# A new order for all queues of a linear-attention layer with a gated MLP, and three dummy matmuls fewer

## The chip, the cores and the metric

The kernel runs on one core of a Trainium2 chip. The metric is the device time of one execution in microseconds (us). A core has five engines that run side by side, each through a queue of its own in order: PE (TensorE, matmuls; PEld is its weight load), ACT (ScalarE), DVE (VectorE), POOL (GpSimd) and SP (SyncE, which issues nearly all the DMAs here).

## The reference

Everything is bf16, with 2048 tokens of 448 features. A layer norm, then attention of 16 heads of 28 features without a token-by-token matrix, the output product and a residual; then a second layer norm and a gated MLP of width 1792 with a residual.

```python
qkv = (layernorm(x) @ wqkv)                       # q, k, v, 16 heads of 28
pq, pk = q @ w_phi[h], k @ w_phi[h]
phi_q = concat([softmax(pq), softmax(-pq)]); phi_k = concat([softmax(pk), softmax(-pk)])
kv, z = phi_k.T @ v, phi_k.sum(tokens)            # per head
o = (phi_q @ kv) / (phi_q @ z + 1e-6)
h = x + o @ wo
out = h + (sigmoid(hn @ w_gate) * (hn @ w_up)) @ w_down     # hn = layernorm(h)
```

## The kernel before

The work is cut into 16 tiles of 128 tokens. `build` records some 900 tasks, each with an engine (or a choice of two or three), the tasks it depends on, and a choice of PSUM banks; the recording order means nothing. A table, `ORDER`, then sets the order of all five queues: each of its numbers names a task (the number over 32), the choice of banks (the next bits) and the choice of engine (the last two). `stored` reads it:

```python
t = self.tasks[names[int(v) // 32]]
t.eng = t.engs[int(v) % 4]
...
t.got, gate = t.banks[int(v) // 4 % 8]
```

A task waits for its dependencies and for whoever last used its banks, by semaphores. `TURNS` adds waits that no data asks for: in each pair the first task also waits for the second, which keeps two tasks of different engines apart.

```python
for name, first in TURNS:
    self.tasks[name].need.append(first)
```

The stages, with the lines that the text speaks of:

- **Start.** `warm` and `fill` (L543, L1006) are dummy matmuls of 512 columns on zeros, which depend on nothing but a cleared tile. `NFILL` says how many there are, and the table where they stand. Four key transpositions on PE (L552) turn the raw key weights; copies (L437, `WkT`) bring them to SBUF; products with the feature weights (L568) fold `w_phi` into the key weights, and copies (`Wk`) bring these to SBUF. The query weights come as four raw loads (`wq_raw`), two DMA transpositions (L512, `WqT`) and the same folding (L568, then `Wq`).
- **First layer norm.** DVE takes statistics (L596, L598). A small step and a power on POOL (L599, L601) make the factor, and `xn_pad` (L614 on ACT, L616 on POOL, L617 on DVE) is the normalized x. Six tiles are transposed by PE (L627) and copied, the others by DMA (L635).
- **Key/value stage.** For each tile 14 + 14 matmuls of half the array (L655), in two tasks of 8 and 6; two exponentials on ACT (L675, L677) and a copy of v; sums and reciprocals (L685 on POOL or DVE, L691, L696, L700); features (L702, `phi`); and 16 short matmuls that add up the summary in bank 4 (L714). L721 starts that accumulation.
- **Query stage.** For each of 4 chunks of 512 tokens and 2 groups, 8 + 6 matmuls (L754) and two exponentials of 1024 columns (L764, `eq`).
- **Output stage.** When the summary is masked (`kvz`, L769), PE makes numerators and denominators of a tile in 16 short matmuls (L790), and ACT or DVE evicts them (L437, `opm`). For a pair of tiles follow, by their lines: reciprocal L806 and ratio L808 on DVE, a multiplication L810 and an addition L813 on `b_sb`, a reciprocal L816, the output multiplication L818 (`o_pad`), all of these big ones on DVE or POOL as the table says. The first pair is transposed by PE (L826, L828), the others get a small copy (L837) and a DMA transposition (L839). Then the output product (L851), the residual addition (L881; for the first pair a matmul adds x, L859, and two copies to `x_sb` follow), statistics (L876 and L878, or L885 and L887), the small step and the power on POOL (L889, L891), the normalization `hn_pad` (L895), and its transposition by PE (L905) or DMA (L913).
- **MLP.** Five token blocks of 2, 4, 4, 4 and 2 tiles. For each of 14 slices of the width, 7 gate and 7 up matmuls (L952), a tanh on ACT (L961), and a product on DVE (L969). Then 14 down matmuls a tile (L986), an addition (L993) and a store (L996).

PSUM has 8 banks. Gate and up, query and output products take pairs of them, so a task of PE also waits until the engines have read what the pair held before.

Of the kernel before, what the change touches and what calls it, by code (L numbers as in the profile page):

```python
# [30 lines left out]
SECOND = [(1, 0), (1, 1), (1, 2), (1, 3), (0, 0), (0, 1), (0, 3)]  # L31
NWARM = 1
KT_MM = 2
NFILL = 20

O_FIRST = [(0, 0), (0, 1), (0, 2), (0, 3), (1, 0), (1, 1), (1, 2)]
O_SECOND = [(1, 0), (1, 1), (1, 2), (1, 3), (0, 0), (0, 1), (0, 2)]
# [1 line left out]


ORDER = """
# [48 lines left out]
"""  # L90


TURNS = [(('Wp', 1), ('Wp', 0)), (('nm', 6), ('ve', 4)), (('mm', 4), ('ve', 4)), (('ve', 12), ('phi', 0)), (('mm',
# [5 lines left out]


class _Task:
# [4 lines left out]
class _Graph:  # L106
# [153 lines left out]
    def emit(self, rings):  # L260
        nc = self.nc
        done = self.stored(ORDER) if ORDER.strip() else self.order()
        for name, first in TURNS:
            self.tasks[name].need.append(first)
# [69 lines left out]
def build(nc, A_x, A_wqkv, A_w_phi, A_wo, B_w_gate, B_w_up, B_w_down, out):  # L334
# [19 lines left out]
    with ExitStack() as es:  # L354
# [649 lines left out]

        for i in range(NFILL):
            task(("fill", i), "pe", 0.22, lambda e: e.matmul(  # L1006
# [40 lines left out]
```

## Time and profile before

| | us |
|---|---|
| median of 3 runs | 204.57 (204.56 to 204.67) |
| the profiled execution | 204.33 |
| its span, first to last instruction | 202.4 |
| busy: PE / DVE / ACT / POOL | 197.8 / 130.4 / 94.1 / 55.0 |
| 20 dummy matmuls (L1006), busy | 8.0 |
| gate and up matmuls (L952), 980 | 175.2 |
| down matmuls (L986), 238 | 43.1 |

Matmuls overlap in the records, so the busy times of the lines add up to more than the stretch they fill. The chain of waits goes back from the last instruction and names at each step what released it. A timeline merges neighbours of one line; its columns are the start, the time from the first start to the last end, the engine, line and operation, and the count; in brackets the idle time ahead and what ended it. The rows that the prediction rests on stand there.

### The profile page before, as it was taken

The page shows a single profiled execution, that of the slowest core. Times are in us where ns is not written, and L with a number is a line of the kernel's source. Part 1 is how long each engine was busy: PE and PEld are TensorE (multiplying, and loading weights), DVE is VectorE, ACT ScalarE, POOL GpSimd, SP SyncE. Part 2 cuts the span into 40 slices and gives each one's busy share as a digit, 9 for nine tenths or more (in the row PEclk, how much of TensorE's full clock was granted, in tenths as well). Part 3 has the DMA queues.
Part 4 walks back from the last instruction along what each step waited for, and adds up shares of the span by engine and source line. Part 5 has one row for each costly group of instructions (what it writes and reads, how often), then busy time and mean ns, then how long its engine had stood idle before and what let it go on. Part 6 is the DMA issues. An engine that isn't in the chain of part 4 may idle for free.

```text
span 202.4 us, 5443 instructions
## 1 busy us (share of the span) xinstructions
PE 197.8 (98%) x2292; PEld 109.8 (54%) x2292; DVE 130.4 (64%) x295; ACT 94.1 (46%) x167; POOL 55.0 (27%) x81
## 2 busy tenths in 40 slices
PE   7999999999999999999999999999999999999994
PEld 2555555555457885555544444454444455896553
DVE  2999999997999898678724448752335224554222
ACT  2599999899998662424221323201352300442000
POOL 4689855442057414344330000300001000000000
PEclk9999999999999999999999999999999999999999
DMA  6996667863025395151371200083000211000111
GB/s 189 328 165 142 162 135 229 242 184 112 0 55 100 63 137 126 25 142 24 83 55 47 52 3 0 0 104 93 0 0 3 52 45 47 3 3 3 45 45 45
DMA packets 34052, 16.67 MB, mean 82 GB/s; under 512 B 25644, under 2 KB 33004, under 8 KB 34028
## 3 DMA queue, kind: packets, MB, share of 16 engines
q1 hardware_dynamic: 33676, 16.04, 34.9%
q8 instruction: 18, 0.29, 0.6%
q10 hardware_dynamic: 352, 0.29, 0.4%
q14 instruction: 6, 0.05, 0.1%
HBM read 8.98 MB, written 1.84 MB: 53 GB/s over the span
## 4 chain that ended last, share of the span: by engine, by line
PE 92%; DVE 2%; ACT 2%; POOL 1%; issue 0%; DVEq 0%
PE bank L952 42%; PE bank L986 21%; PE bank L655 11%; PE bank L851 5%; PE bank L754 4%; PE bank L1006 3%; ACT eq L764 2%; PE bank L714 2%; PE bank L790 1%; PE bank L568 1%; PE bank L627 1%; POOL b_sb L810 1%; PE bank L552 1%; DVE b_sb L813 1%; ACT opm L437 0%
## 5 line engine op out<-in xcount | busy, mean ns | idle before, releaser
L952 PE MATMUL bank<-xnT,wg_sb 64*128 64x512 bf16 (+1 forms) x490 | 87.6, 333 | 0.3 <-issue 0.3
L952 PE MATMUL bank<-xnT,wu_sb 64*128 64x512 bf16 (+1 forms) x490 | 87.6, 333 | 0.0
L961 ACT ACTIVATE sg_sb<-bank 128x512 f32<-128x512 f32 (+1 forms) x70 | 34.4, 512 | 81.2 <-PE bank L952 69.8
L969 DVE SCALAR_TENSOR_TENSOR hh<-sg_sb,bank 128x512 bf16<-128x512 f32 (+1 forms) x70 | 38.8, 576 | 28.3 <-ACT sg_sb L961 28.1
L952 PEld LDWEIGHTS bank<-xnT,wg_sb 64*128 64x128 bf16 x490 | 45.2, 94 | 19.0 <-issue 2.8
L952 PEld LDWEIGHTS bank<-xnT,wu_sb 64*128 64x128 bf16 x490 | 45.0, 94 | 16.8
L986 PE MATMUL bank<-wd_sb,hh 128*128 128x448 bf16 (+2 forms) x238 | 43.1, 342 | 0.0
L986 PEld LDWEIGHTS bank<-wd_sb,hh 128*128 128x128 bf16 x238 | 22.4, 98 | 20.7 <-issue 1.1
L993 DVE SCALAR_TENSOR_TENSOR x_sb<-bank,x_sb 128x448 bf16<-128x448 f32 (+2 forms) x17 | 10.1, 597 | 28.3 <-PE bank L986 28.3
L655 PE MATMUL bank<-Wk,xnT 64*128 64x448 bf16 x112 | 20.4, 350 | 0.0
L655 PE MATMUL bank<-Wv,xnT 64*128 64x448 bf16 x112 | 20.2, 350 | 0.0
L764 ACT ACTIVATE eq<-bank 128x1024 bf16<-128x1024 f32 x16 | 16.0, 1036 | 0.2
L889 POOL TENSOR_SCALAR rs<-mv 128x2 f32<-128x2 f32 x6 | 1.2, 193 | 52.3 <-DVE mv L887 48.7
L754 PE MATMUL bank<-xnT,Wq 64*128 64x512 bf16 x112 | 13.8, 376 | 0.3 <-ACT opm L437 0.3
L851 PE MATMUL bank<-wo_sb,oT 64*128 64x448 bf16 x112 | 13.3, 350 | 0.1
L437 ACT CAST opm<-bank 128x960 bf16<-128x960 f32 x13 | 12.2, 962 | 0.1
L818 POOL TENSOR_TENSOR o_pad<-b_sb,rden 128x896 bf16<-128x896 bf16 x5 | 8.4, 1689 | 12.1 <-DVE rden L816 9.2
L685 POOL TENSOR_TENSOR half_s<-ek 128x448 f32<-128x448 bf16 x10 | 9.7, 970 | 7.6 <-DVE phi L702 5.0
L655 PEld LDWEIGHTS bank<-Wk,xnT 64*128 64x128 bf16 x112 | 8.7, 94 | 5.2 <-issue 0.7
L596 DVE BATCH_NORM_STATS2 st<-x_sb 128x6 f32<-128x448 bf16 x16 | 9.1, 613 | 3.2 <-DMA x_sb<-in_A_x_dram 3.2
L655 PEld LDWEIGHTS bank<-Wv,xnT 64*128 64x128 bf16 x112 | 8.7, 94 | 4.5
L881 DVE TENSOR_TENSOR x_sb<-bank,x_sb 128x896 bf16<-128x896 f32 x7 | 7.6, 1089 | 3.7 <-PE bank L851 3.6
(99 smaller groups left out, 210.3 us busy)
## 6 DMA issues: line engine op xcount, KB each, us to landing
wg_sb<-in_B_w_gate_dram SPq DMA_DIRECT2D x4, 448.0 KB, 4.2
wu_sb<-in_B_w_up_dram SPq DMA_DIRECT2D x4, 448.0 KB, 3.6
out_dram<-x_sb SPq DMA_DIRECT2D x15, 112.0 KB, 1.7
wd_sb<-in_B_w_down_dram SPq DMA_DIRECT2D x7, 224.0 KB, 2.8
x_sb<-in_A_x_dram SPq DMA_DIRECT2D x2, 448.0 KB, 5.1
x_sb<-in_A_x_dram SPq DMA_DIRECT2D x3, 224.0 KB, 3.9
wq_raw<-in_A_wqkv_dram SPq DMA_DIRECT2D x4, 128.0 KB, 4.7
Wv<-in_A_wqkv_dram SPq DMA_DIRECT2D x2, 224.0 KB, 4.2
```

Of the source, the lines that this page charges most:

```text
L437: return e.copy(dst, src) if hasattr(e, "activation") else e.tensor_copy(dst, src)
L596: task(("bst", t), "dve", dve(D), lambda e, t=t: e.bn_stats(st1[:, t % 4, :], X(t)), [x_ld[t], opt(("agg", t - 4))])
L655: r = e.matmul(bank[bk][:, 0:D], lhsT=half(xnT, hi)[:, t, k, :], rhs=half(w, hi)[:, k, :], start=(i == 0), stop=(i == 6), tile_position=(6 ...
L685: task(("sa", t), None, 0.88, lambda e, t=t, s=s: e.tensor_tensor(half_s[:, t % NSA].rearrange("p (a n) -> p a n", a=4 * G), ek[:, s].rear ...
L754: r = e.matmul(bank[bb[j]], lhsT=half(Wq2, hi)[:, k, 2 * g:2 * g + 2].rearrange("p c d h -> p (c d h)"), rhs=half(xnT, hi)[:, 4 * c:4 * c ...
L764: task((key, gp, c), "act", act_p(1024), lambda e, gp=gp, c=c, sg=sg, nm=nm: e.activation(eq[c][:, sg, 2 * gp:2 * gp + 2, :], wide[got(nm) ...
L851: r = e.matmul(bank[bb[j]][:, 0:D], lhsT=half(oT, hi)[:, pr % NO, j, k, :], rhs=half(wo_sb, hi)[:, k, :], start=(i == 0 and not res), stop ...
L952: r = e.matmul(bank[b][:, 0:N], lhsT=half(w, hi)[:, k, fs], rhs=half(hnT, hi)[:, t0:t0 + n, k, :], start=(i == 0), stop=(i == 6), tile_pos ...
L961: task(("sig", f_, c), "act", act_p(N), lambda e, j=j, N=N, nm=nm: e.activation(sg_sb[:, j % NSG, 0:N], bank[got(nm)[0]][:, 0:N], ACT.Tanh ...
L969: task(("hh", f_, c), "dve", dve(N), lambda e, j=j, N=N, nm=nm, f_=f_, c=c: e.scalar_tensor_tensor(hhT[c % 2][:, f_, 0:N], sg_sb[:, j % NS ...
L986: r = e.matmul(bank[b][:, c0:c1], lhsT=hhT[c % 2][:, f_, o:o + P], rhs=wd_sb[:, f_, c0:c1], start=(f_ == 0), stop=(f_ == FT - 1))
L993: task(("fin",) + nm[1:], "dve", dve(c1 - c0), lambda e, nm=nm, tt=tt, pr=pr, c0=c0, c1=c1: e.scalar_tensor_tensor(X(tt)[:, c0:c1], bank[g ...
```

## The change

`NFILL` goes from 20 to 17, and the tables `ORDER` and `TURNS` are replaced as a whole. No task's own code changes. One line of the file goes, so that every line behind the tables has a number smaller by one after the change.

```diff
-NFILL = 20
+NFILL = 17
...
 ORDER = """
-448 0 736 544 224 1152 96 288 576 29120 608 480 28960 640 128 160 28576 800 256 28672 192 768 29024 704 28608
...
+128 448 0 736 544 224 160 1152 96 256 576 28768 608 192 384 480 28992 640 352 28544 768 28960 288 704 28832
...
-TURNS = [(('Wp', 1), ('Wp', 0)), (('nm', 6), ('ve', 4)), (('mm', 4), ('ve', 4)), (('ve', 12), ('phi', 0)), (('mm',
...
+TURNS = [(('Wp', 0), ('Wp', 1)), (('xn', 10), ('mm', 12)), (('sa', 6), ('sa', 4)), (('sa', 8), ('sa', 9)), (('sa',
+         10), ('phi', 9)), (('sa', 11), ('phi', 8)), (('phi', 13), ('phi', 11)), (('c', 0), ('b', 0)), (('b', 2),
+         ('od', 1)), (('b', 3), ('od', 2)), (('o', 3), ('hn', 2)), (('b', 5), ('od', 3)), (('rstd2', 2), ('ve2', 2)),
...
```

In `TURNS`, `b`, `c`, `o` and `od` are the multiplication, the addition, the output multiplication and the small copy of a pair of tiles, and `hn` a normalized tile; `(('b', 2), ('od', 1))` holds the third pair's multiplication until the second pair's copy is done.

What the table moves on the queues, at the places where the prediction speaks of it:

PE's queue where the last key/value tiles give way to the query groups, before (`xnT,Wq` is a query group, `v,phi` the summary, `kvz,eq` a tile's numerators):

```order
L754 MATMUL bank<-xnT,Wq 128x512 x8
L655 MATMUL bank<-Wk,xnT 128x448
L655 MATMUL bank<-Wv,xnT 128x448
L655 MATMUL bank<-Wk,xnT 128x448
L655 MATMUL bank<-Wv,xnT 128x448
L655 MATMUL bank<-Wk,xnT 128x448
L655 MATMUL bank<-Wv,xnT 128x448
L714 MATMUL bank<-v,phi 64x58 x16
L754 MATMUL bank<-xnT,Wq 128x512 x34
L714 MATMUL bank<-v,phi 64x58 x96
L754 MATMUL bank<-xnT,Wq 128x512 x8
L790 MATMUL bank<-kvz,eq 128x60 x32
```

The same place after the change:

```order
L654 MATMUL bank<-Wk,xnT 128x448
L654 MATMUL bank<-Wv,xnT 128x448
L753 MATMUL bank<-xnT,Wq 128x512 x36
L713 MATMUL bank<-v,phi 64x58 x16
L753 MATMUL bank<-xnT,Wq 128x512 x6
L713 MATMUL bank<-v,phi 64x58 x80
L753 MATMUL bank<-xnT,Wq 128x512 x8
L789 MATMUL bank<-kvz,eq 128x60 x32
```

Before, the first half of the group stood ahead of the last key/value half tile, and the run of 34 began with the 6 matmuls that end it. Now the run of 36 is 8 of the first group, 8 of the second, then the 6 that end the first, the 6 that end the second, and 8 of the third.

POOL's queue from the last features to the second power, before:

```order
L702 TENSOR_TENSOR phi<-ek,rsum 128x16x56
L810 TENSOR_TENSOR b_sb<-opm,rr 128x928
L818 TENSOR_TENSOR o_pad<-b_sb,rden 128x2x448
L889 TENSOR_SCALAR rs<-mv 128x2
L891 TENSOR_TENSOR rs<-rs,neghalf 128x2
L810 TENSOR_TENSOR b_sb<-opm,rr 128x928
L813 TENSOR_TENSOR b_sb<-b_sb,opm 128x928
L818 TENSOR_TENSOR o_pad<-b_sb,rden 128x2x448
L889 TENSOR_SCALAR rs<-mv 128x2
```

And after:

```order
L701 TENSOR_TENSOR phi<-ek,rsum 128x16x56 x2
L812 TENSOR_TENSOR b_sb<-b_sb,opm 128x928
L809 TENSOR_TENSOR b_sb<-opm,rr 128x928
L812 TENSOR_TENSOR b_sb<-b_sb,opm 128x928
L888 TENSOR_SCALAR rs<-mv 128x2
L890 TENSOR_TENSOR rs<-rs,neghalf 128x2
L809 TENSOR_TENSOR b_sb<-opm,rr 128x928
L812 TENSOR_TENSOR b_sb<-b_sb,opm 128x928
L888 TENSOR_SCALAR rs<-mv 128x2
```

The first pair's addition, and the third pair's multiplication and addition, now stand ahead of the first power; the first pair's multiplication and the third pair's output multiplication have gone to DVE.

DVE's queue from the first normalization of the output stage to the first residual addition, before:

```order
L895 TENSOR_SCALAR hn_pad<-x_sb,mv,rs 128x512 x2
L806 RECIPROCAL rSm<-opm 128x32
L437 COPY xnT<-bank 128x512 x2
L808 TENSOR_TENSOR rr<-rSm,opm 128x32
L881 TENSOR_TENSOR x_sb<-bank,x_sb 128x896
```

And after:

```order
L894 TENSOR_SCALAR hn_pad<-x_sb,mv,rs 128x512 x2
L817 TENSOR_TENSOR o_pad<-b_sb,rden 128x2x448
L807 TENSOR_TENSOR rr<-rSm,opm 128x32
L836 COPY o_pad<-o_pad 128x2x64
L436 COPY xnT<-bank 128x512 x2
L880 TENSOR_TENSOR x_sb<-bank,x_sb 128x896
```

The third pair's output multiplication and copy now come between the normalization and the copies of its transposed tiles. The two copies of the first pair to `x_sb`, which ACT made, are DVE's now.

Elsewhere: the clearings of the padding (L459, L460, L458, L468 and L469) and the mask of the summary (L464) now stand on POOL ahead of the first small step; all four folded key weights are copied by ACT, where one was DVE's; the small loads of the output weights and the stores stand later on SP.

101 rows, old and new, of tables (ORDER, TURNS) are left out of this document.

## The prediction

> **What bounds the kernel now.** I read the page first, then the waits of PE, then the chain of waits, and then the timelines of the stages in which the chain leaves PE.
>
> ```profile
> span 202.4 us, 5443 instructions
> PE 197.8 (98%) x2292; PEld 109.8 (54%) x2292; DVE 130.4 (64%) x295; ACT 94.1 (46%) x167; POOL 55.0 (27%) x81
> PE bank L754 <- ACT opm L437: 0.3, 1, 0.3
> PE bank L790 <- DVE opm L437: 0.2, 1, 0.2
> ```
>
> PE is busy for 98% of the span, and its waits after the first matmul add up to 0.8 us: these two, and one of 0.3 that term 4 shows. The real work of PE is the same in both versions, so the time after is the time before, less the dummies, less the waits that go, plus the waits that come. The profiled execution took 204.33 us, 1.93 us more than its span, and the median of the runs, 204.57, is 0.24 us above it. I sum against 204.33 and add 0.24.
>
> A busy PE hides how little slack its neighbours have. Three places hold PE up, or nearly: the arrival of the transposed query weights near 18 us, the first gate and up matmul at 61.59, and the second token block at 76.76.
>
> **Term 1, the dummies.** The first run of them shrinks from 12 to 11, those between the key transpositions and 20 us from 4 to 3, and those of the output stage (46 to 62 us) from 4 to 3.
>
> ```profile
> 1.44 5.30 PE L1006 MATMUL bank<-warm 128*128 128x512 bf16 x12
> 6.56 1.76 PE L552 MATMUL bank<-ident,wk_raw 128*128 128x128 bf16 x16
> 8.65 0.22 PE bank L1006
> L473 SPq DMA_DIRECT2D wk_raw<-in_A_wqkv_dram x1: 456/456/456, 1.3 to 1.3; - x1
> DMA to landing us min/median/max: 4.1/4.2/4.3
> ```
>
> The first 12 stand (6.56 - 1.44)/12 = 0.427 us apart; a later one costs 0.22. The key weights are there at 1.3 + 4.3 = 5.6 us, so PE begins the key transpositions 0.43 earlier, and all three dummies are worth at most 0.43 + 0.22 + 0.22 = 0.87 us. What is late next is this:
>
> ```profile
> L512 SPq DMA_TRANSPOSE WqT<-wq_raw x2: 1240/1291/1342, 12.0 to 15.5; - x2
> DMA to landing us min/median/max: 2.7/3.6/4.4
> 18.34 0.75 PE bank L568 x12
> 25.06 0.57 PE bank L655 x6
> 10.14 0.20 PE bank L721
> 9.52 0.20 PE bank L568 x4
> 22.41 0.30 PE bank L568 x4
> ```
>
> The second transposition of the query weights is issued at 15.5 and lands 2.7 later, at 18.2; the product that needs it starts at 18.34. In either order the last of their four raw loads stands behind both big x loads, and only one small row load of the output weights has gone from ahead of it, so I leave the landing where it is. Up to this product PE has nearly the same work behind it in both versions: the new order has the second half of a key/value tile more (0.57), one x transposition (four short matmuls: 0.20) and the accumulator's starting matmul (0.20) fewer, and carries one dummy (0.22) past it, +0.05 for what follows. PE therefore only comes earlier to a wait. **I take 0 for all three dummies** (the one of the output stage goes from a stretch in which PE waits anyway). The bounds are 0.87 gained, if every gate moves along, and 0.1 lost.
>
> **Term 2, the second query projection.** PE now runs both first halves of the next two query groups before it finishes the first.
>
> ```profile
> 40.38 3.84 PE L754 MATMUL bank<-xnT,Wq 64*128 64x512 bf16 x34
> 41.40 5.99 ACT L764 ACTIVATE eq<-bank 128x1024 bf16<-128x1024 f32 x6
> 47.39 2.70 ACT L437 CAST opm<-bank 128x960 bf16<-128x960 f32 x3
> ```
>
> Before, the six matmuls that end the first group are the head of the run at 40.38 (34 matmuls in 3.84 us: 0.11 each), so it is done at about 41.2, and ACT starts its exponentials at 41.40. Now 8 matmuls of another group (0.87) stand ahead of that end. On the way from 18.34 there are three fewer changes between matmuls of the half array and of the full one, at about 0.1 each (four products took 0.20 at 9.52 among their like, and 0.30 at 22.41 where such a change follows): -0.28. With the 0.05 of term 1, ACT starts its six exponentials at 41.2 + 0.87 - 0.28 + 0.05 = 41.85, **0.45 late**. They run back to back, so the evictions behind them start 0.45 late too. Bounds: 0.2 earlier, if the dummies' time survives, and 0.9 late, if the four summary matmuls that now stand in one block ahead of the first query's end wait for their features.
>
> **Term 3, what POOL does before the second normalization.** This decides when the first gate and up matmul can start.
>
> ```profile
> 55.10 0.63 DVE L810 TENSOR_TENSOR b_sb<-opm,rr 128x928 bf16<-128x928 bf16 x1
> 55.66 0.18 DVE L837 COPY o_pad<-o_pad 128x128 bf16<-128x128 bf16 x1
> 56.88 1.69 POOL L818 TENSOR_TENSOR o_pad<-b_sb,rden 128x896 bf16<-128x896 bf16 x1 [6.03 <-DVE rden L816]
> 58.93 0.71 POOL L891 TENSOR_TENSOR rs<-rs,neghalf 128x2 f32<-128x2 f32 x1
> 61.51 1.74 POOL L810 TENSOR_TENSOR b_sb<-opm,rr 128x928 bf16<-128x928 bf16 x1 [1.87 <-DVE rr L808]
> 63.33 1.85 POOL L813 TENSOR_TENSOR b_sb<-b_sb,opm 128x928 bf16<-128x928 bf16 x1
> 59.68 0.74 DVE L895 TENSOR_SCALAR hn_pad<-x_sb,mv,rs 128x512 bf16<-128x512 bf16 x2 [0.19 <-POOL rs L891]
> 60.59 0.74 DVE L437 COPY xnT<-bank 128x512 bf16<-128x512 bf16 x2
> 61.59 0.61 PE bank L952 x8
> ```
>
> Now POOL multiplies and adds (1.74 and 1.85) for the third pair of tiles ahead of the power, where it had one multiplication of 1.69. An entry of the turns holds the first of the two back until DVE's small copy (55.66) is done. That copy comes 0.55 earlier, since its neighbour at 55.10 has left DVE, but the reciprocal list ahead of it waits as long as before: POOL now has the addition (1.85) where it had the multiplication (1.74). So: copy done near 55.4; 1.74 + 1.85 and three gaps of 0.08 end at 59.25; the small step before the power and its gap (0.27) and the power (0.71) bring the normalization to 60.4, **0.75 later** than 59.68. On DVE an output multiplication (0.61) and a copy (0.10) now stand between it and the copies of the first transposed tiles, and one reciprocal (0.26) has gone: **+0.4**. With term 2 the first gate matmul starts 0.45 + 0.75 + 0.4 = 1.6 later, at 63.2. In the meantime PE has done two numerator blocks that used to come later (0.23 each, below), so that the net is **+1.15**. Bounds: 0.1, if ACT's list covers most of it, and 1.6.
>
> ```profile
> 62.20 0.23 PE bank L790 x16
> ```
>
> ACT speaks for a delay of that size by itself. Up to the eviction that frees PE's banks for the second output projection it had five evictions and two half-size copies behind the exponentials, and now has seven evictions:
>
> ```profile
> 56.63 0.53 ACT L437 CAST x_sb<-bank 128x448 bf16<-128x448 f32 x1
> ...
> 57.90 0.56 ACT L437 CAST x_sb<-bank 128x448 bf16<-128x448 f32 x1
> 58.97 0.92 PE L851 MATMUL bank<-wo_sb,oT 64*128 64x448 bf16 x8
> ```
>
> From 56.63 to the end of the second copy this took 1.83; three evictions in a row take 2.70 in the row at 47.39. With term 2 that is 0.87 + 0.45 = 1.3 of delay at PE's 58.97.
>
> **Term 4, the second token block.** Its chain ends in a wait today:
>
> ```profile
> 71.21 3.69 SPq L913 DMA_TRANSPOSE xnT<-hn_pad  x2
> 76.51 0.25 issue
> 76.76 7.73 PE bank L952 x70
> ```
>
> The two transpositions go out back to back, and PE waits 0.25 for the second, some 0.4 with the drain ahead of it. In the new order the first goes out well before the second, and PE comes later, so this wait goes: **-0.4**. A new one comes in the first block: the second residual addition on DVE (1.09 in the row below) now stands behind two normalizations that wait for POOL's multiplication, addition and power in a row, and PE's fifth pair of gate and up groups needs its banks. I put that wait at **+0.3**; nothing and 0.8 are its ends.
>
> ```profile
> L881 DVE TENSOR_TENSOR x_sb<-bank,x_sb 128x896 bf16<-128x896 f32 x7 | 7.6, 1089 | 3.7 <-PE bank L851 3.6
> ```
>
> Behind 76.76 PE runs with no wait in the list above, has the same work and the same number of array changes in both, and the last products, additions and stores are the same. Stores moved behind the last transposition lie beside 10 us of matmuls. I take 0.
>
> **Clearings.** The clearing of the features' padding moves to where DVE waits for x.
>
> ```profile
> 6.70 0.80 DVE L617 TENSOR_SCALAR xn_pad<-x_sb,mv,rs 128x512 bf16<-128x512 bf16 x1
> 7.48 0.40 DVE L617 TENSOR_SCALAR xn_pad<-x_sb,mv,rs 128x512 bf16<-128x512 bf16 x1
> 6.61 0.74 POOL L460 MEMSET phi<- 128x768 bf16 x1
> ```
>
> The first normalization took 0.80 beside this clearing and the second 0.40 without it, so 0.40 of DVE comes back. PE is not waiting for it here, with the dummies ahead, so it is 0 in the sum (bounds: 0.4 gained, 0). The Trainium skill (SBUF — State Buffer, Who interferes with whom) says that VectorE and GpSimd hold a shared pair of ports as an exclusive lock for a whole instruction, and the 0.80 agrees. The same rule speaks against other parts of the new layout, and that is the third rival.
>
> **Sum.** 0 + 1.15 - 0.4 + 0.3 = +1.05 (term 2 is in the 1.15): 204.33 + 1.05 + 0.24 = 205.6; the ends found for term 3 lean low, so I say **205.5**.
>
> **The rivals.**
> - *The dummies' time survives (faster).* If the query weights land earlier with PE, since their loads lose a neighbour, then ACT's exponentials start 0.2 early instead of 0.45 late. It decides at PE's 18.34: starting by 17.7 it holds. Then 0.87 and the 0.4 of term 4 go, and what POOL adds hides behind ACT: 204.33 - 1.27 + 0.24 = 203.3; with half of it, 203.9. Against it: the landing hangs on a DMA chain that the change hardly touches. Chance 0.2.
> - *The output stage is slack (no difference).* PE's dummies and waits there are about 2 us before, and the new delays of POOL and ACT overlap instead of adding. The late start of 0.45 is eaten by the wait that term 4 loses: 204.57. Against it: before, the normalization waits for POOL in the row itself, so POOL's list sets the end. Chance 0.17.
> - *POOL and DVE block each other more (much slower).* A meeting costs DVE 0.4 in the rows above. The long block of feature products on DVE now stands beside three normalizations on POOL, and the adding and multiplying of the output stage beside DVE's own. Three meetings on the path are 1.2, on top of the sum: 206.8. By the skill's lock rule each could cost the whole of POOL's instruction. Chance 0.15.
>
> **How the numbers follow.** The forecast, 205.0 to 206.2, has 0.48. The range of 8 in 10 runs from 203.7, which leaves the lower half of the first rival out, to 206.6, which leaves most of the third out. Faster by over 0.2% (0.4 us, about what a measurement of this kernel can tell from no change) has 0.21, within 0.2% has 0.17, slower 0.62.
>
> **What would show it.** Term 1: the row of the first query weight product again near 18.3, now with a wait of about 0.5 ahead of it. Term 2: the run of six exponentials starting near 41.9. Term 3: the power of the first pair ending near 60.9 with an addition right ahead of it on POOL, and the first gate row near 63.2. Term 4: no wait at the second block's first row, and that row near 77.8. The forecast is wrong if the six exponentials start before 41.3, or if the first gate row comes before 62.

## The result, and the profile after

The new kernel takes 204.98 us (median of 22 runs, 204.65 to 205.77) where the kernel before took 204.59 on the same chip. The ratio is 1.003, with a 95% interval of 1.002 to 1.0039: slower by 0.4 to 0.8 us, while the medians lie 0.39 apart. One of the 22 runs of before took 1150 us and is not in the ratio. 205.5 was predicted, 203.7 to 206.6. The profiled execution is one of the longer ones, 205.08 for a span of 203.1, as the one of before (204.33) was one of its shorter, so the two profiled executions lie 0.75 apart, more than the medians. The page's span and busy times after:

```profile
span 203.1 us, 5436 instructions
PE 197.8 (97%) x2289; PEld 109.4 (54%) x2289; DVE 130.5 (64%) x296; ACT 92.1 (45%) x163; POOL 57.7 (28%) x84
```

PE's waits behind the first matmul (total, count, longest):

```profile
PE bank L789 <- ACT opm L436: 0.4, 1, 0.4
PE bank L904 <- DVE hn_pad L894: 0.3, 1, 0.3
PE bank L1005 <- DVE opm L436: 0.2, 1, 0.2
```

PE is as long busy as before, 197.8, though it has three matmuls fewer. What it lost hides in busy rows. The timeline of PE in the first half (start, length of the stretch, engine, operation, count):

```profile
11.09 0.92 PE L654 MATMUL bank<-Wk,xnT 64*128 64x448 bf16 x8
12.02 0.62 PE L626 MATMUL bank<-ident,xn_pad 128*128 128x128 bf16 x8
17.78 0.37 PE L567 MATMUL bank<-Wp,WqT 112*128 112x112 bf16 x4
24.36 1.84 PE L713 MATMUL bank<-v,phi 128*64 128x58 bf16 x64
26.14 0.82 PE L753 MATMUL bank<-xnT,Wq 64*128 64x512 bf16 x6
46.03 1.04 PE L753 MATMUL bank<-xnT,Wq 64*128 64x512 bf16 x8
```

The first query weight product stands at 17.78, 0.56 earlier than before. What PE waits for ahead of it is named by two steps of the chain of waits, the normalization of a tile on POOL and its transposition on PE:

```profile
12.55 0.78 POOL xn_pad L615
...
13.37 0.40 PE bank L626 x4
```

The feature products of four tiles then take 1.78 up to the next row, with matmuls that wait inside the row; below, the same 64 take 1.13 where nothing is waited for. VectorE's features, which they need, come one after another:

```profile
22.45 1.15 DVE L701 TENSOR_TENSOR phi<-ek,rsum 128x896 bf16<-128x896 bf16 x1
24.02 1.69 DVE L701 TENSOR_TENSOR phi<-ek,rsum 128x896 bf16<-128x896 bf16 x3
```

They end at 25.71. From there on the new kernel is late: by 0.73 at ScalarE's six exponentials (41.40 before), by 0.24 at what follows them (47.63; 47.39 before), and by 0.18 at PE's row at 46.03 (45.85 before). ScalarE's timeline:

```profile
42.13 5.61 ACT L763 ACTIVATE eq<-bank 128x1024 bf16<-128x1024 f32 x6 [0.66 <-PE bank L753]
47.63 0.96 ACT L436 CAST opm<-bank 128x960 bf16<-128x960 f32 x1
```

The chain of waits in the output stage, and behind it the timeline of DVE beside it:

```profile
55.75 1.75 POOL b_sb L809
...
57.57 1.85 POOL b_sb L812
...
59.50 0.20 POOL rs L888
...
59.78 0.72 POOL rs L890
...
60.52 0.73 DVE hn_pad L894 x2
61.26 0.54 DVE o_pad L817
```

```profile
57.24 0.62 DVE L436 CAST x_sb<-bank 128x448 bf16<-128x448 f32 x1 [0.51 <-PE bank L850]
57.79 1.15 DVE L875 BATCH_NORM_STATS2 st<-bank 128x6 f32<-128x448 f32 x2
58.85 0.30 DVE L877 BATCH_NORM_AGGREGATE mv<-st 128x2 f32<-128x6 f32 x2
```

PE's wait of 0.3 at L904 in the list above is the transposition that needs this normalization. And PE's timeline at the first gate row, at the place that waits for the second residual addition, and at the second token block:

```profile
62.29 0.40 PE L789 MATMUL bank<-kvz,eq 64*128 64x60 bf16 x16
62.83 0.27 PE L951 MATMUL bank<-xnT,wg_sb 64*128 64x256 bf16 x1
...
68.22 0.39 PE L789 MATMUL bank<-kvz,eq 64*128 64x60 bf16 x16
68.66 0.28 PE L951 MATMUL bank<-xnT,wg_sb 64*128 64x256 bf16 x1
...
77.24 0.27 PE L951 MATMUL bank<-xnT,wu_sb 64*128 64x256 bf16 x1
77.57 0.37 PE L951 MATMUL bank<-xnT,wg_sb 64*128 64x512 bf16 x1
```

First gate row 1.24 late, with two numerator blocks more behind it (0.23 each): 0.78 net. A numerator block costs 0.23 in steady flow; the one at 68.22 has 0.44 to the next row, so 0.2 of waiting there. At the second block 0.33 instead of 0.11, a wait of 0.2 (0.4 before). The block begins 0.81 late, and the last matmul ends at 200.35 instead of 199.72: **+0.63**. The missing 0.18 comes back behind the second block, which takes 122.78 up to the last matmul and took 122.96 before. It does so in all ten profiles with the new second half (122.76 to 122.78; 122.94 to 122.96 in the four with the old one); the cause is open.

### The profile page after: what moved, and what is told of

It reads as the page before. It is cut to its first block, busy times and chain, and to the rows that moved or that the text cites. A ratio compares the mean times of both kernels' runs of the same rounds, so it can differ in the third digit from the quotient of the medians.

```text
span 203.1 us, 5436 instructions
## 1 busy us (share of the span) xinstructions
PE 197.8 (97%) x2289; PEld 109.4 (54%) x2289; DVE 130.5 (64%) x296; ACT 92.1 (45%) x163; POOL 57.7 (28%) x84
## 4 chain that ended last, share of the span: by engine, by line
PE 77%; DVE 10%; POOL 5%; ACT 4%; DMA 2%; issue 1%; DVEq 0%; POOLq 0%
PE bank L951 40%; PE bank L985 21%; PE bank L654 8%; PE bank L850 3%; ACT eq L763 3%; DMA x_sb<-in_A_x_dram 2%; PE bank L753 2%; PE bank L713 1%; DVE st L595 1%; DVE x_sb L880 1%; POOL b_sb L812 1%; POOL b_sb L809 1%; DVE phi L701 1%; DVE o_pad L817 1%; POOL xn_pad L615 1%
## 5 line engine op out<-in xcount | busy, mean ns | idle before, releaser
L951 PEld LDWEIGHTS bank<-xnT,wu_sb 64*128 64x128 bf16 x490 | 45.5, 94 | 15.5
L763 ACT ACTIVATE eq<-bank 128x1024 bf16<-128x1024 f32 x16 | 15.5, 1049 | 0.7 <-PE bank L753 0.7
L684 POOL TENSOR_TENSOR half_s<-ek 128x448 f32<-128x448 bf16 x9 | 8.6, 968 | 7.3 <-DVE half_s L684 5.5
L812 POOL TENSOR_TENSOR b_sb<-b_sb,opm 128x928 bf16<-128x928 bf16 x4 | 7.4, 1844 | 7.1 <-DVE b_sb L809 6.1
L809 POOL TENSOR_TENSOR b_sb<-opm,rr 128x928 bf16<-128x928 bf16 x4 | 7.0, 1741 | 8.2 <-DVE o_pad L836 5.8
```

The source lines that it names most:

```text
L763: task((key, gp, c), "act", act_p(1024), lambda e, gp=gp, c=c, sg=sg, nm=nm: e.activation(eq[c][:, sg, 2 * gp:2 * gp + 2, :], wide[got(nm) ...
L812: task(("c", pr), None, dve(464), lambda e, both=both, s2=s2: e.tensor_tensor(b_sb[:, s2].rearrange("p t g e j -> p t g (e j)"), b_sb[:, s ...
L951: r = e.matmul(bank[b][:, 0:N], lhsT=half(w, hi)[:, k, fs], rhs=half(hnT, hi)[:, t0:t0 + n, k, :], start=(i == 0), stop=(i == 6), tile_pos ...
```

## Experiments

All edits are in the order table. Steps are named as the code records them, with their indices: `qa` and `q` are the 8 and the 6 matmuls of a query group (second index: the chunk of 512 tokens), `kv` a tile's feature products, `hT` an MLP pair's DMA transposition. Line numbers in these kernels are smaller by four than in the new one. "Late" and "early" are against the profile of the kernel named.

**1. Three dummies out of the old order** (one of the first run, one before the key weight products, one of the output stage).

```diff
-NFILL = 20
+NFILL = 17
```

> The kernel before with three dummies fewer (one of the twelve ahead of the key transpositions, one of the four behind them, one of the four of the output stage), everything else in the old order. Theory of the prediction (the gain ends at the transposed query weights, which land at 18.25): first query weight product again at 18.3, a wait of 0.4 to 0.6 ahead of it, total within 0.2 of the kernel before. Rival (the dummies' time survives): first query weight product by 17.7 and a total 0.6 to 0.9 lower.

Measured: 204.61 against 204.76, ratio 0.9993 (0.9978 to 1.0008). PE's timeline in this kernel:

```profile
1.44 3.68 PE L1001 MATMUL bank<-warm 128*128 128x512 bf16 x11
5.78 0.87 PE L547 MATMUL bank<-ident,wk_raw 128*128 128x128 bf16 x8 [0.66 <-DMA wk_raw<-in_A_wqkv_dram]
10.38 0.93 PE L650 MATMUL bank<-Wv,xnT 64*128 64x448 bf16 x8
11.53 0.62 PE L622 MATMUL bank<-ident,xn_pad 128*128 128x128 bf16 x8 [0.22 <-POOL xn_pad L611]
18.30 0.70 PE L563 MATMUL bank<-Wp,WqT 112*128 112x112 bf16 x11
```

The dummies are worth nothing, as forecast, but not for the reason given. PE is 0.78 early at the key transpositions (part of it by a chance told at the end), there waits 0.66 for the key weights, is 0.28 early at the first value matmuls (10.38; 10.66 before), and then waits again, for POOL's normalized tile. Its next row stands at 11.53 in both kernels. From there to the query weight product PE runs with no wait that a row shows (6.77 here, 6.81 before), and the transposed query weights, which landed at 17.93, are not what it waits for. The ratio's interval leaves room for a gain of up to 0.45.

**2 and 3. New first half with old second half, and the reverse.** The cut is at the row at 46 us, on all queues; the dummy of the output stage goes with its half (18 and 19 dummies).

```diff
-ORDER = old
+ORDER = new[:at(qa, 0, 3)] + [s for s in old if s not in new[:at(qa, 0, 3)]]   # second
+ORDER = old[:at(qa, 0, 3)] + [s for s in new if s not in old[:at(qa, 0, 3)]]   # third
```

> The new order of all queues up to the fourth group of query products (46 us in the profile), the old order behind it. Theory (the new kernel gains 0.56 up to the first query weight product, gives it back in the feature products that wait for DVE's features, and stands 0.18 behind at 46 us): total 0.1 to 0.3 above the kernel before. Rival 1 (the whole loss arises in the output stage): no difference or 0.2 faster. Rival 2 (the whole loss arises ahead of 46 us, through the late exponentials): 0.4 to 0.7 slower.

> The old order up to the fourth group of query products, the new order behind it. Theory (numerators, the third pair's multiplication and addition on POOL and the half-size copies on DVE cost 0.4 to 0.6, of which 0.2 come back at the second token block): 0.3 to 0.5 above the kernel before, first gate matmul near 62.4. Rival 1 (the output stage is slack): no difference. Rival 2 (as the new kernel or worse): 0.6 or more.

Measured: the new first half 205.21 against 204.76, ratio 1.0022 (1.0006 to 1.0039); the new second half 204.55 against 204.76, ratio 0.9996 (0.9986 to 1.0006). In the runs the loss comes with the first half. The median of the second kernel, 0.45 slower, is the second rival of its expectation, but the interval (0.1 to 0.8) holds the theory's 0.1 to 0.3 too. For the third kernel the theory (0.3 to 0.5 slower) missed, and the first rival, no difference, is what the runs show. PE's timeline with the new first half, and behind it the first gate row with the new second half:

```profile
19.11 0.36 PE L563 MATMUL bank<-Wp,WqT 112*128 112x112 bf16 x4 [1.28 <-DMA WqT<-wq_raw]
25.67 1.20 PE L709 MATMUL bank<-v,phi 128*64 128x58 bf16 x64
26.80 0.39 PE L749 MATMUL bank<-xnT,Wq 64*128 64x512 bf16 x2
```

```profile
62.66 0.27 PE L947 MATMUL bank<-xnT,wg_sb 64*128 64x256 bf16 x1
```

In this execution of the same first half the query weights landed at 18.97 instead of 16.80. PE waited 1.28 for them, and then the feature products ran in 1.13 with no wait: one gate has taken the other's place, and at 46 us this kernel stands at 46.51. The profile of the third kernel does not look like its runs: it shows the first gate row 1.07 late (0.61 with the two blocks taken off) although its first half is the old one, and its last matmul 0.23 late (199.95).

**4. Three dummies back into the new order**, at the matching places.

```diff
-NFILL = 17
+NFILL = 20
```

> The new kernel with three dummies put back at the matching places (head, behind the key transpositions, output stage). Theory (the feature products of the first four tiles wait for DVE's features at 24 to 26 us, so what PE loses ahead of them is only less waiting): within 0.2 of the new kernel, the waits inside these products shrink from about 0.6 to about 0.1. Rival (the new order has no wait that swallows them): 0.6 to 0.9 above the new kernel.

Measured: 205.14 against 204.76, ratio 1.0024 (1.0013 to 1.0036), the new kernel's within the intervals. So the dummies are worth nothing there either, as forecast. But the wait in the feature products shrank by 0.17 only (1.61 for the 64, where 1.78 was), not to 0.1: PE waited less further ahead, at the key weights, and stands at 11.98 at the normalized tiles where the new kernel stands at 12.02. PE's timeline:

```profile
1.45 3.96 PE L1001 MATMUL bank<-warm 128*128 128x512 bf16 x12
5.83 0.78 PE L547 MATMUL bank<-ident,wk_raw 128*112 128x128 bf16 x7 [0.42 <-DMA wk_raw<-in_A_wqkv_dram]
```

**5 to 8. Single edits of the new first half, and all three together.**

```diff
 # 5, PE
-(qa,1,1) (qa,1,0) (q,1,1) (q,1,0)
+(qa,1,1) (q,1,1) (qa,1,0) (q,1,0)
 # 6, PE
-(qa,0,0) (kv,0) (kv,1) (kv,2) (kv,3) (q,0,0)
+(qa,0,0) (q,0,0) (kv,0) (kv,1) (kv,2) (kv,3)
 # 7, SP (wom,5: a row load of the output weight; wq: query weights)
-(wq,2) (wom,5) (wq,0) (wq,3) (wqT,0)
+(wq,2) (wq,0) (wq,3) (wom,5) (wqT,0)
```

> The new kernel with one pair of steps exchanged on TensorE: the six matmuls that end the first half of the second query group stand ahead of the eight that begin its other half, as in the kernel before. Theory (the prediction's term 2: ScalarE's six exponentials wait for these matmuls, and their late start reaches the end): exponentials start 0.5 to 0.7 earlier than the new kernel's 42.13, total 0.3 to 0.6 below the new kernel. Rival (ScalarE catches up later anyway, since it hands two half-size copies to VectorE): exponentials as early, total within 0.15 of the new kernel.

> The new kernel with the six matmuls that end the first query group ahead of the feature products of the first four tiles instead of behind them, so that these products come 0.65 later and find VectorE's features ready. Theory (the wait of 0.66 in the feature products is where the dummies' time went, and it reaches the end): the wait falls to 0.15 or less, total 0.3 to 0.6 below the new kernel. Rival (the time is lost again at the exponentials or in the output stage): the wait falls, total within 0.15 of the new kernel.

> The new kernel with one load of the output weight (issue of 1.18 on SyncE) behind the last two query weight loads instead of ahead of them, so that the transposed query weights can be asked for about 1.2 earlier. Theory (in part of the executions the transposed query weights land late, at 19.0 instead of 16.8, and then PE waits for them, in the others VectorE's features set the pace): landing by 17.6 in the profile, total 0 to 0.3 below the new kernel with less spread between the runs. Rival (their landing never matters): no difference at all.

> The new kernel with all three edits: query matmuls exchanged, first feature products 0.65 later, query weight loads earlier. Theory (each of the waits in the first half reaches the end): 0.6 to 1.1 below the new kernel, that is 0.2 to 0.7 below the kernel before. Rival (the output stage ends at the same time whatever comes ahead of it): within 0.2 of the new kernel.

Measured against 204.34: 205.37, ratio 1.0051 (1.0033 to 1.007); 205.06, 1.0041 (1.0022 to 1.0059); 205.04, 1.0038 (1.0022 to 1.0055); 205.35, 1.0057 (1.0035 to 1.0078). None is shown to be faster than the new kernel (1.003), and the theories of all four missed; kernel 7 is its rival's "no difference". In it the landing came at 17.20, as its theory said, but neither the total nor the spread of the runs (204.66 to 205.98) fell. Edit 5 also brought a cost of its own. The timeline of ACT in kernel 8, which has all three edits, and behind it that of PE in kernel 6:

```profile
41.41 1.02 ACT L759 ACTIVATE eq<-bank 128x1024 bf16<-128x1024 f32 x1
43.16 4.84 ACT L759 ACTIVATE eq<-bank 128x1024 bf16<-128x1024 f32 x5 [0.73 <-PE bank L749]
47.95 0.96 ACT L432 CAST opm<-bank 128x960 bf16<-128x960 f32 x1
```

```profile
23.97 1.93 PE L749 MATMUL bank<-xnT,Wq 64*128 64x512 bf16 x14
25.83 1.20 PE L709 MATMUL bank<-v,phi 128*64 128x58 bf16 x64
```

The first exponential came 0.72 early, and what follows the six 0.32 late. A `q` waits until the `qa` of its own group has left the array (`after=nm`, L761). With something between them, 8 and 6 take 0.86 and 0.65; right behind each other `qa` takes 1.09 to 1.10 up to the `q`. Edit 5 puts two such pairs together (2 x 0.23), edit 6 one. Four `qa` and `q` in the order "both first halves, then both second halves" avoid it, which is what the new order does. In kernel 6 the feature products run without a wait (1.16 for the 64, 0.62 less), but PE came later to them: the query weights landed at 18.24, 1.4 after the new kernel's. So this run does not separate the wait from the landing.

**9 and 10. The second query weight transposition held until the first has landed; besides, `q` behind the first tile's feature product.**

```diff
 # 9: edit 7 and
+TURNS.append((wqT,1), (wqT,0))
 # 10: 9 and on PE
-(kv,0) (kv,1) (kv,2) (kv,3) (q,0,0)
+(kv,0) (q,0,0) (kv,1) (kv,2) (kv,3)
```

> The new kernel, with the load of 1.18 behind the query weight loads again, and with the second transposition of the query weights held back until the first has landed. Theory (where two transpositions go out back to back, they land 3.6 to 4.8 after their issue in most profiles instead of 2.7, and this spread of the landing between 16.8 and 19.2 is what makes the new first half slower than the old one): both land 2.7 to 2.9 after their issue, the second near 17.8; the runs lie within 0.5 of each other instead of 1.1, total 0.2 to 0.3 below the new kernel. Rival (the landing is no matter, VectorE's features set the pace): same median as the new kernel, same spread.

> The same kernel, and besides the six matmuls that end the first query group stand behind the feature product of the first tile, ahead of those of the next three tiles, so that neither they nor the products wait for a step just ahead of them. Theory (with a steady landing the wait in the feature products is what is left of the dummies' time, 0.66 less two array changes of 0.1): 0.3 to 0.5 below the kernel with the held transposition alone. Rival (that time is lost again further on): no difference to it.

Measured against 204.49: 206.18, ratio 1.0091 (1.0061 to 1.012), runs from 205.79 to 207.78; and 206.35, ratio 1.0089 (1.0066 to 1.0113). Both missed. The transpositions of kernel 9 by their tile (issue shortest/median/longest in ns, first and last start), and behind it the product in PE's timeline:

```profile
L507 SPq DMA_TRANSPOSE WqT<-wq_raw x2: 1342/1980/2617, 12.4 to 15.3; - x2
DMA to landing us min/median/max: 2.8/3.4/3.9
```

```profile
19.30 0.36 PE L563 MATMUL bank<-Wp,WqT 112*128 112x112 bf16 x4 [1.74 <-DMA WqT<-wq_raw]
```

Held apart, the second still took 3.9, and its issue alone 2.6. In kernel 10 the first took 4.56 with the second not yet issued. So the neighbour is not what makes them slow, and that theory falls. What the two kernels do show is the price of a late landing (19.17 and 19.47): at 46 us they stand at 46.70 and 47.23, where 0.3 of the 0.53 between them is the landing. Over the executions of the new first half with PE's order unchanged (new kernel, 7, 4, 2, 9) the landing came at 16.80, 17.20, 17.78, 18.97, 19.17, PE's product at 17.78, 17.52, 17.92, 19.11, 19.30, and the row at 46 us at 46.03, 45.77, 45.99, 46.51, 46.70. Up to 17.78 no cost of the landing is seen at 46 us. In the last three PE's product follows the landing by 0.13 to 0.14. With the old first half (kernels 11, 3, 12, 1, before) landings of 17.21 to 18.25 gave 18.19 to 18.34, and 45.80 to 45.92.

**11. In kernel 3, the second pair's transposition held so that it goes out back to back with the third's.**

```diff
-(hT,1) (oT,3) (wd,2) (hT,2)
+(oT,3) (wd,2) (hT,1) (hT,2)
+TURNS.append((hT,1), (hn,4))
```

> The kernel with the old order in the first half and the new one in the second, whose twelve runs lay within 0.21 of each other, with one edit: the transposition of the second pair of MLP tiles is held back until the third pair's can go out too, so that the two go out back to back as in the kernel before. Theory (it is the back-to-back pair that spreads the landing, and with it the time of the kernel before): the runs spread over 0.6 or more again, landings 3.2 to 4.4 after their issue, a wait of 0.3 to 1.0 at the second token block, median 0.3 to 1.0 higher. Rival (the spread of the kernel before comes from elsewhere): spread as narrow as before this edit, median within 0.2.

Measured: 205.25 against 204.49, ratio 1.0036 (1.0023 to 1.0049). PE's timeline at the second token block:

```profile
78.09 0.37 PE L947 MATMUL bank<-xnT,wg_sb 64*128 64x512 bf16 x1 [0.88 <-issue]
```

A wait of 0.88 appears there, and the last matmul ends 0.92 later than in kernel 3: nothing behind 77 us absorbs a late start of that block. The price is as forecast, the mechanism is not. The two transpositions went out at 73.61 and 75.14 and landed 2.7 and 2.9 later, not 3.2 to 4.4: the block waits because the second was issued late. And the runs stayed within 0.32 of each other, so the spread theory is refuted.

**12. In the old order, the second pair's power and normalizations ahead of the third multiplication, its transposition ahead of the third output one.**

```diff
 # POOL
-(o,3) (ve2,1) (rstd2,1)
+(ve2,1) (rstd2,1) (o,3)
 # DVE
-(h,2) (bst2,5) (od,3) (bst2,4) (agg2,5) (hh,5,0) (hh,0,0) (rr,5) (hh,6,0) (hh,7,0) ... (hn,2) (hn,3)
+(h,2) (hn,3) (hn,2) (bst2,5) (hh,5,0) (hh,0,0) (od,3) (rr,5) (hh,6,0) (hh,7,0) (bst2,4) (agg2,5) ...
 # SP
-(oT,3) (wd,2) (hT,1) (hT,2)
+(hT,1) (oT,3) (wd,2) (hT,2)
-TURNS: (rstd2,1) behind (od,3)
```

> The kernel before with one part of the new order alone: the power, the normalizations and the transposition of the second pair of MLP tiles go ahead of the third multiplication of the output stage (on GpSimd, VectorE and SyncE), so that this transposition leaves some 3 earlier and not back to back with the next one. Theory (term 4 of the prediction: PE waits at the second token block for the two transpositions, 0.41 in the profile of before, and what this takes from VectorE is hidden): no wait there, second block's first row near 76.3, total 0.2 to 0.5 below the kernel before, below both kernels, and the runs within 0.4 of each other. Rival (the wait has a new cause at once, the later statistics of the third pair or the residual addition): within 0.15 of the kernel before.

Measured: 204.57 against 204.45, ratio 1.001 (0.9996 to 1.0024). The timeline of PE's second block, and of DVE and POOL at the moved steps:

```profile
76.60 0.37 PE L947 MATMUL bank<-xnT,wg_sb 64*128 64x512 bf16 x1
...
67.19 1.26 DVE L890 TENSOR_SCALAR hn_pad<-x_sb,mv,rs 128x512 bf16<-128x512 bf16 x2
...
66.29 1.69 POOL L813 TENSOR_TENSOR o_pad<-b_sb,rden 128x896 bf16<-128x896 bf16 x1
```

The wait is gone, 76.60 instead of 76.76 in the profile, but the runs show no difference: the rival. In the profile too most of the 0.41 is lost again: PE comes to the block 0.24 later than before (76.59 and 76.35), 0.17 of it in small waits of the first block (126 gate and up matmuls in 6.99 instead of 6.88, and 0.29 instead of 0.23 for the numerators behind them). The two normalizations, 0.73 before (at 70.45), take 1.26 beside the multiplication on POOL. No kernel tried is shown to beat the kernel before.

## Why the prediction was right, and where not

The direction held, and in the profile so did the kind of mechanism: the new order gives PE's dummies to other waits, and what it moves on POOL and DVE makes the first gate row late. The size was too large: 205.5 said, 204.98 measured, at the lower edge of the forecast's 205.0 to 206.2. And the direction is in part luck. In the runs the loss comes with the first half, for which the prediction had only ACT's late list. The output stage, from which the larger part of its sum came, shows no loss in the runs of kernel 3.

*Term 1, dummies (0 said).* The amount is right, by kernels 1 and 4. The step to it failed. "PE therefore only comes earlier to a wait" meant the landing at 18.2, and that is the gate in the profile of neither order: in the old one it is POOL's normalized tile at 11.5, and the new one reaches the product at 17.78, not near 18.3, with no wait. There three gates follow each other: the normalized tiles (12.02, just behind ACT's, which ends at 11.97, and 13.37, behind POOL's, which ends at 13.32), the landing when it is late, VectorE's features at 25.7. I took a coincidence for a wait: 18.25 and 18.34 lie 0.09 apart, but no wait row stood there. At most 0.1 is hidden: the last matmul ahead of the product starts 0.38 before it, and 0.28 before it in the new kernel.

*The first rival* said that the time survives if PE starts this product by 17.7. In kernel 7 it starts at 17.52, and the exponentials still start at 41.87, not at 41.2. The features hold it back (they end at 25.45 there, and the 64 products take 1.78 again); the rival named one gate where there are three.

*Term 2 (six exponentials at 41.85, said later as near 41.9).* 42.13, with the 0.28 more coming from the first half. One step of the sum was miscounted: between the product and these six matmuls the traces show 9 changes of the array before and 7 after, two fewer and not three, so that the sum gives 41.93. But the late start is not a loss by itself. "They run back to back, so the evictions behind them start 0.45 late too" failed: before, the merged row of six hid two stops. The second exponential starts 1.09 behind the first, whose end it waits for, and the third 1.13 behind the second, while the others follow at 0.91; that is 0.4 in all. The chain of waits shows that the third waits for PE:

```profile
40.45 3.15 PE bank L754 x28
43.60 0.02 issue
43.62 3.77 ACT eq L764 x4
```

In the new kernel the six follow each other without a stop, and the work behind them starts 0.24 late only. Kernel 8 shows the reverse, an early first and a late last.

*Term 3 (normalization at 60.4, with term 2 in it the first gate at 63.2; net +1.15).* The steps as listed (59.25 + 0.27 + 0.71) end at 60.23, not 60.4, so some 0.15 of the forecast was a slip. With term 2 in it the power was to end near 60.9; it ends at 60.49, the first gate stands at 62.83, net 0.78, of which 0.18 is the first half's. What stands on DVE between the normalization and the gate cost the 0.4 that was said (2.31 from 60.52, 1.91 from 59.68 before). For the rest the mechanism is half right. The chain of waits names POOL's multiplication and addition, as forecast, and POOL's small step starts at 59.50. But the statistics that it needs end at 59.15 (58.85 + 0.30), 0.9 later than before's 58.23 (58.05 + 0.18), since a copy that ACT made stands ahead of them on DVE, behind a late output product. With POOL idle the step could have begun near 59.25, an estimate from that end and the 0.09 that POOL takes between its steps: POOL's list is worth 0.25, and the rest I had not seen.

*Term 4 (-0.4 and +0.3).* The wait at the second block fell by 0.2 instead of 0.4, since the third pair's transposition took 3.6 from issue to landing (77.48); the wait for the second residual addition came, 0.2. The sum was right to 0.1. Kernel 12 says the first part is worth nothing in the old order. Behind the second block 0 was said, and the new order is 0.18 shorter there.

*The second rival* (the output stage is slack) is not ruled out: the runs of kernel 3 (204.55 against 204.76) fit it, its profile (first gate row 0.61 late, last matmul 0.23 late) does not.

*Where the loss sits.* The profiles and the runs agree on the first half, within a wide interval. At 46 us the four executions of the new order above in which no transposition was held (new kernel, 7, 4, 2) average 46.08, the five of the old 45.88, so 0.2, and the runs of kernel 2 say 0.45 (0.1 to 0.8). That the features and the landing make this loss is read from the rows: no kernel that took one of them away became faster. The profiles and the runs do not agree on the second half. From 46 us to the last matmul the old order took 153.87, 153.45 and 153.80 (before, kernels 1 and 2), the new 154.32, 154.03, 154.36 and 154.30 (after, 3, 4 and 7): 0.5 more. The runs of kernel 3 show 0.3 less to 0.1 more. **That stays open.** Its twelve runs lie between 204.45 and 204.66, the 35 of before beside them between 204.14 and 205.14, and every profile of the old order at hand is of a short run (204.33, 204.0, 204.14). All twelve are longer than the shortest of before and shorter than its median (204.76), so a profile of a short run of before makes the new second half look worse than the median does. What makes the long runs of before long was not found; kernels 11 and 12 rule out the back-to-back transpositions.

*The third rival* (POOL and DVE block each other) did not decide. The moved clearing did what was said: the first normalization took 0.38 instead of 0.80, and no effect on the end can be seen. A meeting cost DVE 0.4 there, beside a clearing of 0.74, and 0.53 in kernel 12 (the first of the two normalizations takes 0.94 instead of 0.41), beside a multiplication of 1.69. Neither cost is the whole of POOL's instruction, which the rival named as a possible price.

## What to carry to other kernels

A wait that the limiting engine avoids is worth what the next gate leaves of it (a gate is any point at which it must wait for another engine or a transfer): look for every gate between the edit and the end, in several executions, before giving a saved dummy a price. Two times that nearly coincide are not a wait; look for a row that says who waited, and split a merged row before calling its steps back to back. And where a chain names one engine, look for a second chain that ends just behind it, since shortening the first gains only the difference.

## What the hardware showed besides

The run of dummies in the new kernel's timeline of PE:

```profile
1.44 4.50 PE L1005 MATMUL bank<-warm 128*128 128x512 bf16 x11
```

- The dummies' own length varies from execution to execution. Eleven took 4.50 in the new kernel (1.44 to 5.95) and 3.68 in kernel 1: 0.427 each at first and 0.216 later, and the change came at 3.6 to 3.9 us in kernels 1 and 4, at 5.3 in the new kernel, and behind all twelve in before. The granted clock in the profile's rows is 1.00 throughout. The Trainium skill (TensorE: Matmul & The Clock Gate, Part 1: The HAM clock gate) says that the array starts at half rate until a free-running window of activity has passed, and that the number of slow matmuls varies from run to run; the traces agree, with 6 to 12 slow ones. So a dummy in the head takes 0.43 or 0.22, by chance, and it is worth nothing to what follows where PE then waits for the key weights (0.66 in kernel 1).
- The two DMA transpositions of the query weights took 2.7 to 4.8 us from issue to landing over these kernels, also where the other one was not in flight (2.7 to 4.6 in kernels 9 and 10).
- Where `q` waits for the `qa` right ahead of it, the next pair of matmuls starts 0.44 to 0.45 after the last instead of 0.21 to 0.22 (kernels 5 and 8), so such a wait costs PE 0.23.
